# A one-token decoder block: wq in one load over all 128 partitions, and the last rows of w_down as two loads of 128 rows

## The chip, the cores and the metric

The kernel runs on one core of a Trainium2 chip. The metric is the device time of one execution in microseconds (us); shorter is better. Everything is stored in bf16; the sums are kept in fp32.

## What is computed

One token with 640 features passes through an attention block with a cache of 4096 positions and 32 heads of 128 features, and then through a gated feed-forward block with 1728 hidden features. `A_x` is x; `B_x` isn't used.

```python
q = (layernorm(x) @ wq)                       # 640 x 4096, 32 heads of 128
p = softmax(q . k_cache * 128 ** -0.5)        # 32 heads, 4096 positions
h = x + (p @ v_cache) @ wo                    # 4096 x 640
g = layernorm(h) @ w_gate                     # 640 x 1728
u = layernorm(h) @ w_up                       # 640 x 1728
out = h + (gelu(g) * u) @ w_down              # 1728 x 640
```

Nearly all of the input is read once: K and V are 33.6 MB each, wq and wo 5.2 MB each, the three matrices of the feed-forward block 2.2 MB each, 84.2 MB in all.

## The kernel before, in words

The program is written as one list of operations for each engine, with explicit dependencies (`Prog`, lines 33 to 90). `P.dma` (line 50) puts a load on the list of the engine that issues it; all but the load of x are issued by SyncE (SP), in the order in which they stand in the code. An operation that depends on another waits on a semaphore (line 84) before it is issued, and everything behind it on that engine waits too. A DMA counts as done when its semaphore has reached 16 (line 90). SP's queue thus holds the loads in a fixed order, and a load that waits for a buffer holds up all those behind it.

**Start.** SP issues wq first (lines 156 to 158), into `arena`, a buffer of 40 KB in each partition. Five successive rows of wq go to one partition, so partition p gets 40,960 contiguous bytes. The load is split in two: partitions 0 to 15 (640 KB) and partitions 16 to 127 (4480 KB). Meanwhile VectorE and GpSimd write constants, and a small layernorm of x is done (lines 212 to 231). The matrix multiply `q_proj` (lines 236 to 243) waits for the layernorm and for both loads of wq; it makes q for all heads, repeated over 32 partitions for each of four heads, and VectorE and ScalarE copy it to `qb` (lines 244 and 245).

**The stream of K and V.** The heads are taken in eight groups of four. K of a group is one load of 4096 KB over 128 partitions (32 partitions for each head, 32 KB a partition), V as well; the last V is in two halves. There are three slots of memory for these loads, and the order is K0, K1, V0, K2, V1, and so on (`order`, lines 159 to 162). `issue` (line 172) puts the next load on SP's list with a wait for the last use of its slot; the first three wait for nothing and are issued behind wq. For each quarter of a K load, VectorE multiplies K by q (line 254), TensorE folds the 128 features to 16 by adding eight slices in PSUM (line 262), VectorE sums those 16 (line 269), and ScalarE takes the exponentials (line 273). TensorE then multiplies them with V (line 291) and adds up the partial sums of the heads (line 300).

**The rest.** When the last K and V loads have been put on the list, SP issues wo in three loads into `arena` (lines 360 to 362), which is free once q is made. The matrices of the feed-forward block go into the slots of the last K and V loads (lines 363 to 378): first the last 192 rows of w_down, in two loads (128 rows into column 12 of `wd_sb`, 64 rows into partitions 0 to 63 of column 13), then w_gate, w_up in two pieces, and the first 1536 rows of w_down in three. The first of them waits for the last use of its slot (`free[1]`).

The hidden features lie in 14 columns of 128: `glu` (line 392) computes gate and up by 5 x 14 matmuls of 128 by 128 each into one column of PSUM at a time; the fourteenth column has 64 features, so its matmuls are half as wide and fill only half of the partitions. Two memsets (lines 380 and 381) put zeros in the other half, since the gelu (lines 414 to 422) works on whole columns. `down` (line 424) multiplies each column by its 128 rows of w_down, or by the 64 rows in the last column, in four quarters of 160 outputs, columns 12 and 13 first, then the others in the order in which they land. Two copies each on VectorE and ScalarE and a store end the program.

Of the kernel before, what the change touches and what calls it, by code (L numbers as in the profile page):

```python
# [92 lines left out]
def bass_sequential_preLN__gqa_block_cached__glu_gated_geglu__decode_kernel(nc, A_x, A_k_cache, A_v_cache, A_wq, A_wo, B_x, B_w_gate, B_w_up, B_w_down, out):  # L93
# [3 lines left out]
    arena = sb("arena", [128, 5 * 4096], BF16)  # L97
# [13 lines left out]
    hlnT = sb("hlnT", [128, 5], BF16)  # L111
# [12 lines left out]
    hm = sb("hm", [128, 14], BF16)  # L124
# [10 lines left out]
    ps_g, ps_u = bank[0], bank[1]  # L135
    ps_q = [bank[3], bank[7]]
    ps_a = bank[3]
    ps_d = bank[3][:, 256:416]
# [8 lines left out]
    P = Prog(nc)  # L147
    V = lambda fn, *d: P.op("vector", fn, *d)
# [4 lines left out]

    d_x = P.dma("scalar", x_row[:, :], A_x[0, :, :])
    A(lambda e: e.preload_act_table_set("natural_log_exp_and_others"))
    wq_v = A_wq[:, :].rearrange("(p c) n -> p (c n)", c=5)
    d_wq = [P.dma("sync", arena[0:16, :], wq_v[0:16, :]),
            P.dma("sync", arena[16:128, :], wq_v[16:128, :])]
    order = [("K", 0)]
    for G in range(NG - 1):  # L160
        order += [("K", G + 1), ("V", G)]
# [86 lines left out]
    folds, reds, exps, pvs, evs, hds = {}, {}, {}, {}, {}, {}  # L248
# [76 lines left out]
    def proj_part(t, lo, hi, *ws):  # L325
        def fn(e):
            for c in range(5):
                for i in range(lo, hi):
                    r = e.matmul(ps_p[:, c:c + 1], wo_sb[:, t, i, c::5], aP[:, t, i:i + 1],  # L329
                                 start=(t == 0 and c == 0 and i == 0), stop=(t == 1 and i == 15),  # L330
                                 skip_group_check=True)
            return r
        return T(fn, *ws)
# [11 lines left out]
    for G in range(NG):  # L345
# [6 lines left out]
        if G == 4:  # L352
# [14 lines left out]
    wd_sb = sl[1][:, 0:14 * D].rearrange("p (m n) -> p m n", m=14)  # L367
# [1 line left out]
    wd_v = B_w_down[0:1536, :].rearrange("(a p r) n -> p a r n", a=3, r=4)  # L369
    wd_d = wd_sb[:, 0:12, :].rearrange("p (a r) n -> p a r n", a=3)  # L370
    d_wd = [P.dma("sync", wd_sb[:, 12, :], B_w_down[1536:1664, :], free[1]),
            P.dma("sync", wd_sb[0:64, 13, :], B_w_down[1664:1728, :])]
    d_wg = P.dma("sync", wg_sb, B_w_gate[:, :].rearrange("(p c) n -> p c n", c=5), free[0])
    d_wu = [P.dma("sync", wu_sb[:, 0:3, :], wu_v[:, 0:3, :]),
            P.dma("sync", wu_sb[:, 3:5, :], wu_v[:, 3:5, :])]
# [1 line left out]
             P.dma("sync", wd_d[:, 2, 0:2, :], wd_v[:, 2, 0:2, :]),  # L377
             P.dma("sync", wd_d[:, 2, 2:4, :], wd_v[:, 2, 2:4, :])]

    V(lambda e: e.memset(ps_g[64:128, 13:14], 0.0), reds[31])  # L380
    V(lambda e: e.memset(ps_u[64:128, 13:14], 0.0), reds[31])
    proj_part(0, 0, 16, a0, d_wo["0"])
    proj_part(1, 0, 12, a1, d_wo["1a"])
    pr = proj_part(1, 12, 16, d_wo["1b"])
# [7 lines left out]
    def glu(ps, w, cs):  # L392
        def fn(e):
            for c in cs:
                for m in range(14):
                    ws = w[:, c, 512 * (m // 4) + m % 4:512 * (m // 4) + 512:4] if m < 12 else \
                        w[:, c, 128 * m:min(128 * m + 128, DF)]
                    k = 128 if m < 13 else 64
                    i = e.matmul(ps[0:k, m:m + 1], ws, hlnT[:, c:c + 1], start=(c == 0 and m == 0), stop=(c == 4),  # L399
                                 skip_group_check=True)  # L400
            return i
        return fn
    ga = T(glu(ps_g, wg_sb, range(5)), hl, d_wg)
# [20 lines left out]
    def down(ms, last):  # L424
        def fn(e):
            for m in ms:
                k = 128 if m < 13 else 64
                for q in range(4):
                    i = e.matmul(ps_d[32 * q:32 * q + 1, 0:160], hm[0:k, m:m + 1],  # L429
                                 wd_sb[0:k, m, 160 * q:160 * q + 160],  # L430
                                 start=False, stop=(last and m == ms[-1]))
            return i
        return fn
# [41 lines left out]
```

## Time and profile before

| | us |
|---|---|
| median of 3 runs | 218.11 (217.61 to 218.71) |
| the profiled execution | 218.02 |
| its span, first to last instruction | 216.2 |

The span is what the profile sees; 1.8 us of the profiled execution's time lie outside it. The views call TensorE's matmuls PE and its weight loads PEld, VectorE DVE, ScalarE ACT and GpSimd POOL; SPq is SyncE's queue of issues. L240 is line 240 of the kernel. A row of the table of stretches has the stretch in us and its length, the busy time and the instructions of each engine, and at its end the clock granted to TensorE, the busy share of the 16 DMA engines, and the GB/s that they moved. In that table a packet's bytes and time are counted in the stretch where it begins. A row of a load has its size in KB (of 1024 bytes) and the us from its issue to its landing.

### The profile page before, as it was taken

To read this page: it belongs to the slowest core of one execution; us is meant where nothing else is said; L and a number is where in the kernel's file an instruction comes from. 1 tells how busy PE (TensorE), PEld (TensorE's weight loads), DVE (VectorE), ACT (ScalarE), POOL (GpSimd) and SP (SyncE) were. 2 spreads that over 40 slices of the span, in tenths; PEclk is the share of its full clock that TensorE was granted. 3 is DMA by queue.
4 is the path that set the end of the run, shared out by engine and by line. 5 is a ranking of instruction groups with operands and counts; after the bars stand their busy time and mean duration, and the time that the engine had idled before them with its cause. 6 is when DMAs were issued, how large, how long until landed. Compare 5 with 4: busy or idle time off the path is not lost.

```text
span 216.2 us, 2508 instructions
## 1 busy us (share of the span) xinstructions
PE 121.3 (56%) x1009; PEld 58.8 (27%) x1009; DVE 100.8 (47%) x104; ACT 61.1 (28%) x273; POOL 4.1 (2%) x12
## 2 busy tenths in 40 slices
PE   1000080573965782498186728846880979566394
PEld 1000020221321240134032413312240326266382
DVE  4100001797786950875379177627923781100221
ACT  2100001056155372046205603630660156100101
POOL 7000000000000000000000000000000000000000
PEclk9999999999699998569969967995899599965555
DMA  9999899999999999999999999999999999999992
GB/s 121 227 250 242 220 436 436 424 443 406 464 396 394 449 418 452 418 436 432 430 430 430 436 415 455 414 430 430 436 430 433 415 418 433 424 405 394 406 403 76
DMA packets 4271, 84.39 MB, mean 390 GB/s; under 512 B 482, under 2 KB 676, under 8 KB 1444
## 3 DMA queue, kind: packets, MB, share of 16 engines
q1 hardware_dynamic: 4258, 84.23, 97.2%
q8 instruction: 8, 0.13, 0.3%
q14 instruction: 3, 0.02, 0.0%
q10 hardware_dynamic: 2, 0.00, 0.0%
HBM read 84.23 MB, written 0.00 MB: 390 GB/s over the span
## 4 chain that ended last, share of the span: by engine, by line
DMA 67%; DVE 14%; PE 13%; issue 3%; SPq 2%; DVEq 0%
DMA slot<-in_A_k_cache_dram 46%; DVE prod L254 12%; DMA slot<-in_A_v_cache_dram 11%; DMA slot<-in_B_w_down_dram 10%; PE bank L262 8%; PE bank L291 3%; DVE sc L269 2%; SPq L51 2%; PE bank L300 1%; PE bank L429 1%; DVEq L445 0%; DVE out_row L438 0%; PE bank L311 0%; DVE RT L310 0%
## 5 line engine op out<-in xcount | busy, mean ns | idle before, releaser
L262 PE MATMUL bank<-prod,id_b 128*128 128x512 bf16 x256 | 75.7, 456 | 53.7 <-DVE prod L254 53.7
L254 DVE TENSOR_TENSOR prod<-slot,qb 128x4096 bf16<-128x4096 bf16 x32 | 72.4, 2285 | 31.5 <-DMA slot<-in_A_k_cache_dram 31.5
L273 ACT ACTIVATE p_bd<-sc,zero_t 32x32 bf16<-32x32 f32 x128 | 46.4, 362 | 88.9 <-DVE sc L269 87.7
L262 PEld LDWEIGHTS bank<-prod,id_b 128*128 128x128 bf16 x256 | 27.0, 113 | 102.8 <-DVE prod L254 66.5
L269 DVE TENSOR_REDUCE sc<-bank 128x32 f32<-128x512 f32 x32 | 22.0, 689 | 21.6 <-PE bank L262 21.5
L273 ACT ACTIVATION_READ_ACCUMULATOR p_bd<-sc,zero_t 32x1 f32 x128 | 23.5, 184 | 0.0
L291 PE MATMUL bank<-slot,p_bd 128*16 128x512 bf16 x256 | 17.3, 380 | 0.4 <-DMA slot<-in_A_v_cache_dram 0.4
L240 PE MATMUL bank<-arena,xlnB 128*32 128x512 bf16 x40 | 4.5, 630 | 23.0 <-DMA arena<-in_A_wq_dram 23.0
L244 DVE CAST qb<-bank 128x512 bf16<-128x512 f32 x1 | 0.7, 692 | 25.9 <-PE bank L240 25.9
L291 PEld LDWEIGHTS bank<-slot,p_bd 128*16 128x16 bf16 x256 | 9.4, 89 | 4.6 <-DMA slot<-in_A_v_cache_dram 0.9
L300 PE MATMUL bank<-po_sb,hs 128*16 128x128 f32 x64 | 8.4, 274 | 1.1 <-ACT po_sb L295 1.1
L329 PE MATMUL bank<-aP,arena 128*128 128x1 bf16 x160 | 6.7, 179 | 3.9 <-DMA arena<-in_A_wo_dram 3.9
L399 PE MATMUL bank<-hlnT,slot 128*128 128x1 bf16 (+1 forms) x140 | 6.7, 176 | 3.5 <-DMA slot<-in_B_w_gate_dram 3.5
L240 PEld LDWEIGHTS bank<-arena,xlnB 128*32 128x32 bf16 x40 | 1.6, 140 | 25.0 <-issue 25.0
L245 ACT CAST qb<-bank 128x512 bf16<-128x512 f32 x1 | 0.6, 586 | 26.4 <-PE bank L240 26.4
L329 PEld LDWEIGHTS bank<-aP,arena 128*128 128x128 bf16 x160 | 6.6, 131 | 4.0 <-DMA arena<-in_A_wo_dram 2.6
L399 PEld LDWEIGHTS bank<-hlnT,slot 128*128 128x128 bf16 (+1 forms) x140 | 6.3, 118 | 4.4 <-issue 4.1
L295 ACT COPY po_sb<-bank 128x512 f32<-128x512 f32 x8 | 4.7, 585 | 7.4 <-PE bank L291 7.4
L300 PEld LDWEIGHTS bank<-po_sb,hs 128*16 128x16 f32 x64 | 5.5, 96 | 4.5 <-issue 2.1
L225 ACT ACTIVATE ln<-ln,eps_t 128x1 f32<-128x1 f32 x2 | 0.6, 294 | 17.0 <-DVE ln L223 17.0
L385 DVE TENSOR_TENSOR hT<-xx,bank 128x5 f32<-128x5 f32 x1 | 0.2, 161 | 10.2 <-PE bank L329 10.2
L315 DVE TENSOR_SCALAR aT<-bank,rz 16x128 bf16<-16x128 f32 x2 | 0.7, 340 | 5.8 <-PE bank L300 5.8
(59 smaller groups left out, 24.6 us busy)
## 6 DMA issues: line engine op xcount, KB each, us to landing
slot<-in_A_k_cache_dram SPq DMA_DIRECT2D x8, 4096.0 KB, 22.2
slot<-in_A_v_cache_dram SPq DMA_DIRECT2D x7, 4096.0 KB, 17.5
arena<-in_A_wq_dram SPq DMA_DIRECT2D x1, 4480.0 KB, 26.7
slot<-in_A_v_cache_dram SPq DMA_DIRECT2D x2, 2048.0 KB, 20.5
arena<-in_A_wo_dram SPq DMA_DIRECT2D x1, 2560.0 KB, 27.3
slot<-in_B_w_gate_dram SPq DMA_DIRECT2D x1, 2160.0 KB, 16.6
arena<-in_A_wo_dram SPq DMA_DIRECT2D x1, 1920.0 KB, 31.5
slot<-in_B_w_up_dram SPq DMA_DIRECT2D x1, 1296.0 KB, 18.4
```

The lines of the kernel that those rows point to most:

```text
L51: ev = self.op(eng, lambda e: e.dma_start(out, in_), *deps, dma=True)
L240: i = e.matmul(ps_q[hf][32 * j:32 * j + 32, :], xlnB[:, c, :], wq_j[:, c, j, 4 * hf:4 * hf + 4, :], start=(c == 0), stop=(c == 4))
L254: m = V(lambda e: e.tensor_tensor(out=prod[:, s % 4, :, :], in0=kt[:, 32 * u:32 * u + 32, :], in1=qb[:, G, :].unsqueeze(1).to_broadcast([1 ...
L262: i = e.matmul(ps_f[s % 2][:, :], id_b[:, :], prod[:, s % 4, :, 16 * b:16 * b + 16], start=(b == 0), stop=(b == 7))
L269: reds[s] = V(lambda e: e.reduce_sum(sc[:, s % 4, :], ps_f[s % 2][:, :].rearrange("p (g d) -> p g d", d=16), axis=AX.X), folds[s], exps.ge ...
L273: x = A(lambda e, j=j: e.activation(p_bd[32 * j:32 * j + 32, G % 2, 32 * (s % 4):32 * (s % 4) + 32, j], sc[32 * j:32 * j + 32, s % 4, :], ...
L291: i = e.matmul(po[a:a + 16, :], p_bd[:, G % 2, 4 * b:4 * b + 4, :].rearrange("p g j -> p (g j)"), vt[:, 4 * b:4 * b + 4, :], start=(b < 4) ...
L295: evs[G] = A(lambda e: e.copy(po_sb[:, G % 2, :], po[:, :]), pvs[G], hds.get(G - 2))
L300: i = e.matmul(ps_a[0:16, 128 * (G // 4):128 * (G // 4) + 128], hs[:, r, 12 - 4 * g:28 - 4 * g], po_sb[:, G % 2, 128 * r:128 * r + 128], s ...
L329: r = e.matmul(ps_p[:, c:c + 1], wo_sb[:, t, i, c::5], aP[:, t, i:i + 1], start=(t == 0 and c == 0 and i == 0), stop=(t == 1 and i == 15), ...
L399: i = e.matmul(ps[0:k, m:m + 1], ws, hlnT[:, c:c + 1], start=(c == 0 and m == 0), stop=(c == 4), skip_group_check=True)
L429: i = e.matmul(ps_d[32 * q:32 * q + 1, 0:160], hm[0:k, m:m + 1], wd_sb[0:k, m, 160 * q:160 * q + 160], start=False, stop=(last and m == ms ...
```

## The change

wq becomes one load over all 128 partitions. The load of the last 64 rows of w_down becomes a load of the last 128 rows (1600 to 1727), so that its first 64 rows are ones that other columns hold already and its last 64, in partitions 64 to 127, are those that are used. The fourteenth column therefore lives in partitions 64 to 127 instead of 0 to 63: the two memsets clear partitions 0 to 63, `glu` writes its narrow matmuls to partitions 64 to 127, and `down` reads `hm` and `wd_sb` there.

```diff
-    wq_v = A_wq[:, :].rearrange("(p c) n -> p (c n)", c=5)
-    d_wq = [P.dma("sync", arena[0:16, :], wq_v[0:16, :]),
-            P.dma("sync", arena[16:128, :], wq_v[16:128, :])]
+    d_wq = [P.dma("sync", arena[:, :], A_wq[:, :].rearrange("(p c) n -> p (c n)", c=5))]
...
     d_wd = [P.dma("sync", wd_sb[:, 12, :], B_w_down[1536:1664, :], free[1]),
-            P.dma("sync", wd_sb[0:64, 13, :], B_w_down[1664:1728, :])]
+            P.dma("sync", wd_sb[:, 13, :], B_w_down[1600:1728, :])]
...
-    V(lambda e: e.memset(ps_g[64:128, 13:14], 0.0), reds[31])
-    V(lambda e: e.memset(ps_u[64:128, 13:14], 0.0), reds[31])
+    V(lambda e: e.memset(ps_g[0:64, 13:14], 0.0), reds[31])
+    V(lambda e: e.memset(ps_u[0:64, 13:14], 0.0), reds[31])
...
-                    k = 128 if m < 13 else 64
-                    i = e.matmul(ps[0:k, m:m + 1], ws, hlnT[:, c:c + 1], start=(c == 0 and m == 0), stop=(c == 4),
-                                 skip_group_check=True)
+                    i = e.matmul(ps[0 if m < 13 else 64:128, m:m + 1], ws, hlnT[:, c:c + 1],
+                                 start=(c == 0 and m == 0), stop=(c == 4), skip_group_check=True)
...
-                k = 128 if m < 13 else 64
+                k = slice(0 if m < 13 else 64, 128)
                 for q in range(4):
-                    i = e.matmul(ps_d[32 * q:32 * q + 1, 0:160], hm[0:k, m:m + 1],
-                                 wd_sb[0:k, m, 160 * q:160 * q + 160],
+                    i = e.matmul(ps_d[32 * q:32 * q + 1, 0:160], hm[k, m:m + 1], wd_sb[k, m, 160 * q:160 * q + 160],
                                  start=False, stop=(last and m == ms[-1]))
```

## The prediction

> **What bounds the kernel now.** I read the profile's first parts, then the chain of waits, then tables of stretches, then the issues of the loads one by one. The busy shares alone look balanced, with no engine near full:
>
> ```profile
> span 216.2 us, 2508 instructions
> PE 121.3 (56%) x1009; PEld 58.8 (27%) x1009; DVE 100.8 (47%) x104; ACT 61.1 (28%) x273; POOL 4.1 (2%) x12
> ...
> DMA  9999899999999999999999999999999999999992
> GB/s 121 227 250 242 220 436 436 424 443 406 464 396 394 449 418 452 418 436 432 430 430 430 436 415 455 414 430 430 436 430 433 415 418 433 424 405 394 406 403 76
> ...
> DMA 67%; DVE 14%; PE 13%; issue 3%; SPq 2%; DVEq 0%
> ```
>
> The DMA row is full from the first slice to the last but one, and the chain that ends last is two thirds transfers. The GB/s row tells what the DMA row hides: in the first five slices (5.4 us each) the DMA engines are just as busy and move half as much. The table of stretches cuts this at the landings:
>
> ```profile
> 0.00:9.30 9.30, 0.96 (x7) 0.78 (x7) 2.77 (x13) 1.87 (x3) 4.11 (x12) 1.00 0.89 141
> 9.30:28.00 18.70, 0.00 (x0) 0.00 (x0) 0.00 (x0) 0.00 (x0) 0.00 (x0) 1.00 0.99 263
> 28.00:37.60 9.60, 4.46 (x40) 1.60 (x40) 0.69 (x1) 0.59 (x1) 0.00 (x0) 1.00 1.01 437
> ...
> 0.00:28.00 28.00, 0.96 (x7) 0.78 (x7) 2.77 (x13) 1.87 (x3) 4.11 (x12) 1.00 0.96 222
> 28.00:162.00 134.00, 85.68 (x506) 35.03 (x506) 81.66 (x61) 49.68 (x231) 0.00 (x0) 0.89 1.00 429
> 185.00:191.00 6.00, 2.39 (x32) 1.20 (x32) 0.58 (x4) 0.58 (x1) 0.00 (x0) 0.99 1.01 427
> 191.00:195.60 4.60, 3.36 (x80) 3.28 (x80) 0.00 (x0) 0.00 (x0) 0.00 (x0) 0.50 0.99 395
> ```
>
> The last three columns are the clock granted to TensorE, the DMA share and GB/s. The slow stretch is that of wq, and it stands on the path: the matrix multiply that makes q waits 23.0 us for it.
>
> ```profile
> arena<-in_A_wq_dram SPq DMA_DIRECT2D x1, 640.0 KB, 8.5
> arena<-in_A_wq_dram SPq DMA_DIRECT2D x1, 4480.0 KB, 26.7
> 1.24 0.40 SPq L51 DMA_DIRECT2D arena<-in_A_wq_dram  x1
> L240 PE MATMUL bank<-arena,xlnB 128*32 128x512 bf16 x40 | 4.5, 630 | 23.0 <-DMA arena<-in_A_wq_dram 23.0
> L244 DVE CAST qb<-bank 128x512 bf16<-128x512 f32 x1 | 0.7, 692 | 25.9 <-PE bank L240 25.9
> ```
>
> Issued at 1.24, the load of 112 rows lands at 27.94. From there on the stream never stops. The chain in order of time shows the first and the last link:
>
> ```profile
> 1.70 35.95 DMA slot<-in_A_k_cache_dram
> ...
> 189.26 22.68 DMA slot<-in_B_w_down_dram
> 211.94 0.04 issue
> ```
>
> K's first group lands at 37.65, 9.71 us after wq, which is what 4096 KB (4.194 MB) take at 429 GB/s, 9.8 us. The last piece of w_down lands at 211.94, and only the last few matmuls, the copies and the store follow.
>
> **Does everything behind wq move with it?** It does if the arithmetic keeps up and no queue runs dry.
>
> ```profile
> L254 DVE TENSOR_TENSOR prod<-slot,qb 128x4096 bf16<-128x4096 bf16 x32 | 72.4, 2285 | 31.5 <-DMA slot<-in_A_k_cache_dram 31.5
> L269 DVE TENSOR_REDUCE sc<-bank 128x32 f32<-128x512 f32 x32 | 22.0, 689 | 21.6 <-PE bank L262 21.5
> 37.67 2.29 DVE L254 TENSOR_TENSOR prod<-slot,qb 128x4096 bf16<-128x4096 bf16 x1 [4.40 <-DMA slot<-in_A_k_cache_dram]
> ```
>
> A group of four heads costs VectorE (72.4 + 22.0)/8 = 11.8 us and the DMA engines 2 x 9.8 = 19.6 us (K and V), and VectorE idles 31.5 us waiting for K. The product q.K of the first group also waits 4.40 us for K, not for q: q is ready 4.5 + 0.7 us after wq lands, and K 9.7 us after it. Each of these distances is counted from the landing of wq, so an earlier landing keeps them. What was done while wq was under way is short: POOL is busy for 4.11 us and VectorE for 2.77 us of the first 9.3 us, and nothing at all runs from there to 28.0. That cover is gone only if wq landed before 9.3 us, and at full rate its 5.243 MB need 12.2 us.
>
> **What the wq edit is worth.** How long one row's packet takes now: 5120 KB in 128 rows are 40,960 bytes each. Packets are counted where they begin.
>
> ```profile
> 1.00:1.70 0.70, 0.00 (x0) 0.00 (x0) 0.51 (x5) 0.35 (x1) 0.70 (x1) 1.00 0.01 2
> ...
> 1.00:2.00 1.00, 0.00 (x0) 0.00 (x0) 0.75 (x6) 0.65 (x1) 0.93 (x2) 1.00 3.65 493
> 2.00:3.00 1.00, 0.35 (x5) 0.27 (x5) 0.47 (x1) 0.63 (x1) 1.00 (x3) 1.00 1.23 164
> ```
>
> The packets that begin from 1 to 3 us carry 493 + 164 = 657 KB, the sixteen rows of the first load, and take (3.65 + 1.23) x 16 engines = 78.1 engine-us: 4.88 us a row. In the stretch 9.3 to 28.0 it is 0.99 x 16 x 18.7 = 296 engine-us for 263 x 18.7 = 4.92 MB, so 2.47 us a row if all were wq rows. At 429 GB/s a row would take 40,960 x 16 / 429 GB/s = 1.53 us. After the change no wq load of 16 or of 112 rows exists; one load of 128 rows is left, eight rows an engine. The trace has no 128-partition load of rows this long. The nearest are K and V, 4096 KB over 128 partitions or 32 KB a partition, at 429 GB/s, and the first half of wo, 20 KB a partition:
>
> ```profile
> 162.11 22.79 DMA slot<-in_A_v_cache_dram
> ...
> 163.67 0.43 SPq L51 DMA_DIRECT2D arena<-in_A_wo_dram  x1
> ...
> arena<-in_A_wo_dram SPq DMA_DIRECT2D x1, 2560.0 KB, 27.3
> ```
>
> It lands at 190.97 behind V's last piece at 184.90, so it fills the stretch from 185 to 191 us, at 427 GB/s. The length of the piece between 20 and 32 KB makes no difference there, so I take 429 for wq's 40 KB too. The lowest rate of a stretch with 128-partition loads alone, 395 (191.0 to 195.6 us), is the other bound, 13.3 us instead of 12.2.
>
> Packets begin at about 1.8 us (almost none before 1.7); that stays. Two ways to count the gain:
> - By landings. wq and K's first group are 9.437 MB, 22.0 us at 429, so K lands at 1.8 + 22.0 = 23.8 instead of 37.65: 13.8 us earlier.
> - By bytes. Up to 28.0 the engines moved 222 x 28.0 = 6.22 MB; at 429 that is done at 1.8 + 14.5 = 16.3: 11.7 us earlier.
>
> They differ because a landing waits for the last of 16 engines while the others are already at the next load. The end of the kernel is also a landing, but 170 us later, by when other delays have mixed the engines. I take the middle, 12.7, and keep both ends.
>
> The saved issue on SP (0.40 us) buys nothing: the three loads behind it wait in the rings anyway. The one load may start as much later as it is longer to issue, 0.4 us by that same row; I count it at nothing, since the K loads of 128 rows are issued at the same price:
>
> ```profile
> 49.37 0.33 SPq L51 DMA_DIRECT2D slot<-in_A_k_cache_dram  x1
> ```
>
> **What the w_down edit costs.** It reads 64 more rows, 80 KB, and moves the 64 useful rows to partitions 64 to 127.
>
> ```profile
> 186.03 0.33 SPq L51 DMA_DIRECT2D slot<-in_B_w_down_dram  x1
> ...
> 186.41 0.53 SPq L51 DMA_DIRECT2D slot<-in_B_w_down_dram  x1
> ...
> slot<-in_B_w_down_dram SPq DMA_DIRECT2D x1, 160.0 KB, 12.1
> slot<-in_B_w_down_dram SPq DMA_DIRECT2D x1, 80.0 KB, 12.2
> 164.14 0.91 SPq L51 DMA_DIRECT2D arena<-in_A_wo_dram  x2
> arena<-in_A_wo_dram SPq DMA_DIRECT2D x1, 640.0 KB, 33.1
> ```
>
> The 128-row load lands at 198.1, the 64-row load behind it at 198.6: 0.5 us for 80 KB. The 128-row load itself came some 0.4 us after the last wo piece (issued about 164.6, landed 197.7), for twice the bytes. So the new load costs between 0.1 us less than the old and, if time goes by rows, 0.5 us more; by bytes, 82 KB at 400 GB/s, 0.2 more. I take +0.2, on the path, since w_gate, w_up and the rest of w_down queue behind it. The wait for the slot is the same one, so nothing new stands on SP. The two memsets keep their shape, and the matmuls of the 14th column keep their number (10 and 4 of the 64-row form) and only change array rows or columns:
>
> ```profile
> L399 PE MATMUL bank<-hlnT,slot x140: 164/172/215, 203.7 to 210.8; 128*128 128x1 bf16 x130, 128*64 128x1 bf16 x10
> L429 PE MATMUL bank<-slot,hm x56: 287/338/342, 211.3 to 213.6; 128*1 128x160 bf16 x52, 64*1 64x160 bf16 x4
> ```
>
> They cost nothing, hidden behind the w_down landing at 211.94; were each of the fourteen 0.05 us slower without that cover, it would be 0.7 us.
>
> Sum: -12.7 + 0.2 = -12.5. The profiled execution took 218.02 us, its span 216.2 and 1.8 around it; it lies 0.1 from the median of 218.11. So 205.5 us. Its own bounds: -13.8 - 0.1 gives 204.1, and -11.7 + 0.5 + 1.1 (the 395 rate) gives 207.9.
>
> **The rivals.** First, only part comes back. Halfway, a row of the one load takes 2.0 us (328 GB/s): 16.0 us instead of 12.2, so 209.3. Further, whatever held the 112-row load at 263 GB/s (its long rows, or where wq lies in memory) holds the one load too: its 5.243 MB take 19.9 us and wq is in at 21.7. By landings K comes at 31.5 (6.1 earlier); by bytes, at 28.0 there are 5.24 + 6.3 x 0.429 = 7.95 MB moved instead of 6.22, worth 4.0. The middle is 5.1, so 213.1 us. For it: the trace has no other load from wq. Against it: the 16-row load was twice as slow from the same tensor with the same rows, so neither sets the time alone. [...]
>
> Second, no change: the 16 engines are busy at 0.96 through the first 28 us whichever load they serve, and if the start of a program is slow by time and not by load, 6.2 MB are moved by 28.0 again and only the w_down bytes change: 218.2 us. Against it: the rate rises exactly where the wq packets end. [...]
>
> Third, slower: which sixteen rows are under way together sets the time of a row (4.88 us for the first sixteen, 2.47 later), and the new sets could be of the bad kind. Eight rows at 4.88 are 39.0 us, wq lands at 40.8, K 9.8 behind it at 50.6, 13.0 later than now: 231.2 us. It turns into a loss from (27.94 - 1.8)/8 = 3.27 us a row. Against it: the long 128-partition loads in the trace run at 395 GB/s or more, and there too sixteen engines have sixteen rows under way.
>
> **How the numbers follow.** The forecast gets 0.74, the halfway case 0.09, the 263 GB/s case 0.07, no change 0.05, slower 0.05. The predicted time is that of the first, 205.5. The range takes the first from its low end (203.9, a little under 204.1 for the spread of runs) and the halfway case, up to 210.0: 0.83. Faster by more than 0.5%, about what a measurement of this kernel can tell from no change, are the first three: 0.90; within it 0.05; slower 0.05.
>
> **What would show it.** In the changed kernel's profile the first stretch should run at some 430 GB/s from 2 us on, the q matmul start near 14.5 us, its wait for wq shrink from 23.0 to about 9, K land near 24 to 25 with VectorE still waiting some 4 us for it, the later groups keep their pitch of 19.6 us, and the last w_down landing come near 199.5. The small w_down load should land 0.4 to 0.5 us after the one before it. I am wrong if wq lands after 16 us (its rate is below 370 GB/s), or if it lands early and the chain then holds a new wait, on VectorE or PE, ahead of K loads.

## The result, and the profile after

The changed kernel takes 205.74 us (median of 4 runs, 205.60 to 206.69) against 218.41 for the kernel before (4 runs beside it): a ratio of 0.943, 95% interval 0.938 to 0.948. The profiled execution took 205.85 us, its span 204.0. The forecast was 205.5 us, inside 203.9 to 210.0.

The same rows of the changed kernel's page that were read before (span, DMA share and GB/s in 40 slices, now of 5.1 us, the chain by engine):

```profile
span 204.0 us, 2507 instructions
...
DMA  7999999999999999999999999999999999999991
GB/s 249 434 442 411 411 488 430 418 411 442 430 430 424 418 427 463 424 419 418 443 450 424 421 424 438 443 430 418 424 434 450 389 440 435 413 409 425 415 393 55
...
DMA 64%; PE 14%; DVE 14%; SPq 4%; issue 3%; DVEq 0%
```

The slow start is gone: the second slice already moves 434 GB/s. The first slice holds the 1.8 us before wq's first packet. The rest looks as before, and so does the tail. The table of stretches, cut at other places (its last three columns are TensorE's clock, the DMA share and GB/s):

```profile
0.00:2.00 2.00, 0.00 (x0) 0.00 (x0) 0.97 (x7) 0.66 (x1) 1.34 (x6) 1.00 0.96 267
2.00:9.30 7.30, 0.95 (x7) 0.77 (x7) 1.80 (x7) 1.22 (x3) 2.78 (x7) 1.00 0.87 370
9.30:14.00 4.70, 0.00 (x0) 0.00 (x0) 0.00 (x0) 0.00 (x0) 0.00 (x0) 1.00 0.97 418
...
16.00:150.00 134.00, 86.52 (x506) 35.41 (x506) 81.88 (x61) 49.82 (x231) 0.00 (x0) 0.85 1.00 430
...
0.00:16.00 16.00, 0.95 (x7) 0.77 (x7) 2.77 (x13) 1.87 (x3) 4.11 (x12) 1.00 0.93 379
...
1.00:3.00 2.00, 0.35 (x5) 0.27 (x5) 1.22 (x6) 1.28 (x1) 1.93 (x4) 1.00 1.17 328
4.00:14.40 10.40, 0.60 (x2) 0.50 (x2) 1.19 (x6) 0.59 (x2) 0.78 (x2) 1.00 1.02 441
```

The same for the 112-row load of the kernel before, from the beginning of its first row to that of its last:

```profile
5.90:24.60 18.70, 0.00 (x0) 0.00 (x0) 0.44 (x1) 0.29 (x1) 0.00 (x0) 1.00 1.03 245
```

A packet is counted where it begins, so a short stretch can show more or less than was moved in it; the last two lines of the first table and the line below it hold whole rounds of packets, in each of which an engine has one row (in the changed kernel sixteen rows begin every 1.51 us, and each takes 1.51). There the time of one row of wq can be read: DMA share x 16 engines x 40.96 KB / GB/s. In the changed kernel the first sixteen rows take 655 x 1.17 / 328 = 2.34 us, the later ones 655 x 1.02 / 441 = 1.52 us. In the kernel before it was 4.88 us for the first sixteen and 655 x 1.03 / 245 = 2.75 us for the 112 behind them. The path behind it:

```profile
16.35 4.05 PE L238 MATMUL bank<-arena,xlnB 128*32 128x512 bf16 x40 [11.27 <-DMA arena<-in_A_wq_dram]
...
1.24 24.66 DMA slot<-in_A_k_cache_dram
...
25.92 2.29 DVE L252 TENSOR_TENSOR prod<-slot,qb 128x4096 bf16<-128x4096 bf16 x1 [4.78 <-DMA slot<-in_A_k_cache_dram]
...
L252 DVE TENSOR_TENSOR prod<-slot,qb 128x4096 bf16<-128x4096 bf16 x32 | 72.4, 2284 | 31.6 <-DMA slot<-in_A_k_cache_dram 31.6
...
201.34 0.10 PEld L426 LDWEIGHTS bank<-slot,hm 128*1 128x1 bf16 x8 [0.40 <-DMA slot<-in_B_w_down_dram]
```

The q matmul starts at 16.35 instead of 28.07, K lands at 25.90 instead of 37.65 (11.75 earlier), VectorE waits for K as long as before (31.6 against 31.5 us in all), and the last eight matmuls wait for the last piece of w_down until 201.34. In the kernel before they waited until 213.52, 12.2 us later:

```profile
213.52 0.10 PEld L429 LDWEIGHTS bank<-slot,hm 128*1 128x1 bf16 x8 [0.38 <-DMA slot<-in_B_w_down_dram]
```

The last piece of V lands 11.8 us earlier (173.08 against 184.90). What was gained at wq thus reaches the end of the stream unchanged, and some 0.4 us more are gained behind V, in the loads of the last weights.

### The profile page after: what moved, and what is told of

The parts are those of the page before. It is cut to its first block, busy times and chain, and to the rows that moved or that the text cites. A ratio compares the mean times of both kernels' runs of the same rounds, so it can differ in the third digit from the quotient of the medians.

```text
span 204.0 us, 2507 instructions
## 1 busy us (share of the span) xinstructions
PE 121.1 (59%) x1009; PEld 58.9 (29%) x1009; DVE 100.9 (49%) x104; ACT 61.1 (30%) x273; POOL 4.1 (2%) x12
## 4 chain that ended last, share of the span: by engine, by line
DMA 64%; PE 14%; DVE 14%; SPq 4%; issue 3%; DVEq 0%
DMA slot<-in_A_k_cache_dram 43%; DVE prod L252 12%; DMA slot<-in_A_v_cache_dram 11%; DMA slot<-in_B_w_down_dram 10%; PE bank L260 10%; SPq L51 4%; PE bank L289 3%; DVE sc L267 2%; PE bank L298 1%; PE bank L426 0%; DVEq L441 0%; DVE out_row L434 0%; PE bank L309 0%; DVE RT L308 0%
## 5 line engine op out<-in xcount | busy, mean ns | idle before, releaser
L252 DVE TENSOR_TENSOR prod<-slot,qb 128x4096 bf16<-128x4096 bf16 x32 | 72.4, 2284 | 31.6 <-DMA slot<-in_A_k_cache_dram 31.6
L242 DVE CAST qb<-bank 128x512 bf16<-128x512 f32 x1 | 0.7, 692 | 13.8 <-PE bank L238 13.8
## 6 DMA issues: line engine op xcount, KB each, us to landing
arena<-in_A_wq_dram SPq DMA_DIRECT2D x1, 5120.0 KB, 15.4
slot<-in_B_w_gate_dram SPq DMA_DIRECT2D x1, 2160.0 KB, 15.4
```

Of the source, the lines that this page charges most:

```text
L242: qa = V(lambda e: e.tensor_copy(qb[:, 0:4, :].rearrange("p g d -> p (g d)"), ps_q[0][:, :]), qd)
L252: m = V(lambda e: e.tensor_tensor(out=prod[:, s % 4, :, :], in0=kt[:, 32 * u:32 * u + 32, :], in1=qb[:, G, :].unsqueeze(1).to_broadcast([1 ...
```

## The experiments

Two questions were open: which of the two edits gives the gain, and why a load over 16 or 112 partitions is slow. The theory was that the partitions of the rows under way at the same time set the rate. The rivals were the number or size of the loads, a cold start, and the place of wq in memory. Single runs stand beside a kernel before of 218.2 to 218.4 us, whose own runs lie between 217.2 and 219.3; where a run has an interval, it is named.

**Each edit alone.** The wq edit alone is the kernel before with one load:

```diff
-    d_wq = [P.dma("sync", arena[0:16, :], wq_v[0:16, :]),
-            P.dma("sync", arena[16:128, :], wq_v[16:128, :])]
+    d_wq = [P.dma("sync", arena[:, :], A_wq[:, :].rearrange("(p c) n -> p (c n)", c=5))]
```

> The wq edit alone. Theory (the gain is wq's alone, and 64 rows more of w_down cost their bytes): wq lands near 16 us, 205.5 us, 0 to 0.4 us below the changed kernel. Rival (the w_down load over 128 partitions takes part in the gain): over 206.5 us.

Measured: 206.41 us, ratio 0.9452 (0.9432 to 0.9473): 12.0 us less than before. It lies between the theory's time and the rival's, 0.7 above the 205.74 of the changed kernel, which were taken on another occasion. The w_down edit alone is the changed kernel with the two old wq loads:

```diff
-    d_wq = [P.dma("sync", arena[:, :], A_wq[:, :].rearrange("(p c) n -> p (c n)", c=5))]
+    d_wq = [P.dma("sync", arena[0:16, :], wq_v[0:16, :]),
+            P.dma("sync", arena[16:128, :], wq_v[16:128, :])]
```

> The w_down edit alone. Theory: wq lands at 28 us as before, 218.6 us, that is 0.2 us above the kernel before (between 0.1 below and 0.5 above). Rival (it takes part in the gain): 217.5 us or less.

Measured: 217.60 us, ratio 0.9974 (0.9954 to 0.9994). By the ratio it is 0.6 us less, by the medians 0.8, and not 0.2 more; the interval ends just below 1, and the time lies a little above the rival's mark. Both results point to a small gain from w_down, so the two versions were run again side by side.

> The changed kernel again, beside the wq edit alone on the same chip. If the w_down edit costs its bytes, it is 0 to 0.4 us above the wq edit alone; if it gains as in the run with the w_down edit alone (0.6 us), 0.4 to 0.8 us below it.

> The wq edit alone again, on the same chip as the changed kernel: 205.3 to 205.7 us if the w_down edit costs its bytes, 206.2 us or more if it gains.

Measured: 205.72 us for both edits (205.49 to 206.25, 5 runs) and 206.22 for wq alone (206.03 to 206.62, 4 runs); their ratios to the kernel before are 0.9428 (0.9398 to 0.9458) and 0.9451 (0.9422 to 0.9480), which overlap. The difference of 0.5 us has the sign of the two earlier ones (0.6 and 0.7), and by the times alone it isn't shown. The profiles show a gain of some 0.3 us. Lines of the chain (V's last piece, the last eight matmuls) and of SP's issues with their us to landing, first of this last pair's run with the 64-row load, then of the one with 128 rows:

```profile
150.92 22.15 DMA slot<-in_A_v_cache_dram
...
201.60 0.46 PE bank L427 x8
...
175.40 0.58 SPq L51 DMA_DIRECT2D slot<-in_B_w_gate_dram  x1
slot<-in_B_w_gate_dram SPq DMA_DIRECT2D x1, 2160.0 KB, 16.2
```

```profile
150.82 22.15 DMA slot<-in_A_v_cache_dram
...
201.21 0.46 PE bank L426 x8
...
174.96 1.03 SPq L51 DMA_DIRECT2D slot<-in_B_w_gate_dram  x1
slot<-in_B_w_gate_dram SPq DMA_DIRECT2D x1, 2160.0 KB, 16.3
```

From V's landing (173.07, 172.97) to w_gate's (191.60, 191.26) it is 18.5 us with 64 rows and 18.3 with 128, for 80 KB more. In the kernel before it was 203.57 - 184.90 = 18.7, in the changed kernel 191.43 - 173.08 = 18.35:

```profile
186.97 1.29 SPq L51 DMA_DIRECT2D slot<-in_B_w_gate_dram  x1
slot<-in_B_w_gate_dram SPq DMA_DIRECT2D x1, 2160.0 KB, 16.6
```

```profile
149.97 23.11 DMA slot<-in_A_v_cache_dram
176.03 0.43 SPq L51 DMA_DIRECT2D slot<-in_B_w_gate_dram  x1
slot<-in_B_w_gate_dram SPq DMA_DIRECT2D x1, 2160.0 KB, 15.4
```

So 0.2 to 0.3 us are gained by the time w_gate lands, and they stay to the end. From V's landing to the last eight matmuls it is 28.6 us in the kernel before and 28.5 in both runs of the wq edit alone, 28.3 in the changed kernel and with the w_down edit alone, and 28.2 in the changed kernel run again: in all six profiles less with 128 rows. The single packets of these traces say where it lies: a row of w_gate takes 0.70 to 0.71 us on average behind the 64-row load and 0.66 behind the 128-row load, which for eight rows an engine is about 0.35 us. Why these rows are slower no run shows, and what the times differ by beyond 0.3 us isn't placed.

**Two loads, but over all partitions.** The sizes 640 and 4480 KB are kept, the cut is by columns:

```diff
+    d_wq = [P.dma("sync", arena[:, 0:2560], wq_v[:, 0:2560]),
+            P.dma("sync", arena[:, 2560:20480], wq_v[:, 2560:20480])]
```

> wq again as two loads of 640 and 4480 KB, but cut by columns: each load goes to all 128 partitions. Theory (the partitions set the rate, not the number or the size of the loads): wq lands at 16 to 16.5 us, 205.7 us. Rival (two loads in a row, or the small first one, are what is slow): wq lands after 20 us, 210 us or more.

```profile
15.80 4.46 PE L240 MATMUL bank<-arena,xlnB 128*32 128x512 bf16 x40 [10.73 <-DMA arena<-in_A_wq_dram]
```

Measured: 205.51 us, wq in at 15.8. The number and the size of the loads are not what was slow. (The time at which wq is in is here and below the start of the q matmul.)

**Half of the partitions at a time:**

```diff
+    d_wq = [P.dma("sync", arena[64 * i:64 * i + 64, :], wq_v[64 * i:64 * i + 64, :]) for i in range(2)]
```

> wq as two loads of 64 rows, partitions 0 to 63 and 64 to 127. [...] Rival (only the 16-row load was held up by its partitions, and 112 or 64 rows are as good as 128): wq lands near 16.5 us, 206 us.

```profile
4.80:25.30 20.50, 0.28 (x2) 0.18 (x1) 0.83 (x3) 0.59 (x2) 0.00 (x0) 1.00 1.08 224
...
29.19 4.17 PE L239 MATMUL bank<-arena,xlnB 128*32 128x512 bf16 x40 [24.11 <-DMA arena<-in_A_wq_dram]
```

Measured: 218.39 us, wq in at 29.2. The direction is the theory's, the size isn't: a row takes 655 x 1.08 / 224 = 3.16 us, not the 2.4 to 2.9 (211 to 215 us for the kernel) that I had worked out from half of 4.88; the half was an estimate of mine. With two equal halves the whole gain is gone.

**Sixteen rows at a time, three ways.** First into 16 partitions in a row, then into 16 partitions eight apart, then into 16 in a row but from rows eight apart in memory:

```diff
+    # 16 in a row
+    d_wq = [P.dma("sync", arena[16 * i:16 * i + 16, :], wq_v[16 * i:16 * i + 16, :]) for i in range(8)]
+    # partitions eight apart
+    d_wq = [P.dma("sync", arena[i::8, :], wq_v[16 * i:16 * i + 16, :]) for i in range(8)]
+    # rows of wq eight apart
+    d_wq = [P.dma("sync", arena[16 * i:16 * i + 16, :], wq_v[i::8, :]) for i in range(8)]
```

> wq as eight loads of 16 rows, each to 16 partitions in a row. [...] Rival (only the first load of a program is slow, since it starts cold): 1.5 us a row from the second load on, wq lands near 19 us, 209 us.

> wq as eight loads of 16 rows, each to 16 partitions that lie eight apart; the rows of a load are neighbours in memory as in the run with 16 partitions in a row. The rows of wq thus land in other partitions than the multiply by q expects: the work is the same, q is another. [...] Rival (the rows' place in memory sets it): 4.9 us a row, wq lands at 38 to 43 us, 229 to 234 us.

> wq as eight loads of 16 rows, each to 16 partitions in a row, but from rows of wq that lie eight apart in memory; rows land in other partitions than the multiply by q expects, so q is another. Theory (the partitions set the rate): 4.9 us a row, wq lands at 38 to 43 us, 229 to 234 us. Rival (the rows' place in memory sets it): 2.9 us a row or less, wq lands before 26 us, below 216 us.

One stretch and the q matmul of each, in the same order:

```profile
6.00:42.30 36.30, 0.00 (x0) 0.00 (x0) 0.44 (x1) 0.19 (x1) 0.00 (x0) 1.00 1.11 126
...
49.13 3.93 PE L239 MATMUL bank<-arena,xlnB 128*32 128x512 bf16 x40 [44.05 <-DMA arena<-in_A_wq_dram]
```

```profile
4.30:25.10 20.80, 0.60 (x2) 0.50 (x2) 0.95 (x4) 0.59 (x2) 0.48 (x2) 1.00 1.07 221
...
28.98 4.02 PE L239 MATMUL bank<-arena,xlnB 128*32 128x512 bf16 x40 [23.90 <-DMA arena<-in_A_wq_dram]
```

```profile
6.00:42.30 36.30, 0.00 (x0) 0.00 (x0) 0.44 (x1) 0.20 (x1) 0.00 (x0) 1.00 1.05 123
...
48.20 4.35 PE L239 MATMUL bank<-arena,xlnB 128*32 128x512 bf16 x40 [43.12 <-DMA arena<-in_A_wq_dram]
```

Measured: 238.26, 218.35 and 237.50 us; wq in at 49.1, 29.0 and 48.2; 5.77, 3.17 and 5.59 us a row. The order of the rows in memory changes a row's time by 3%, the partitions change it by almost half, and a cold start is ruled out, since the slow rows go on through 42 us. All three are slower than expected (229 to 234, 211 to 215 and 229 to 234 us), since a row in the long run takes more than the first sixteen rows of a program did (4.88 us).

**Another source, same partitions.** The two old loads read the K cache in place of wq:

```diff
+    wq_v = A_k_cache[0, 0:5, :, :].rearrange("h s d -> (h s d)").rearrange("(p n) -> p n", p=128)
```

> The kernel before, but the two loads to partitions 0 to 15 and 16 to 127 read the first five heads of the K cache in place of wq, 40,960 bytes a partition as before; wq is left out, so q is another. Theory (the partitions set the rate, whatever is read): the loads land at 28 us, 218.4 us. Rival (wq itself, where it lies in memory, is slow unless it is read in one load): they land before 20 us, below 211 us.

```profile
9.30:25.00 15.70, 0.00 (x0) 0.00 (x0) 0.00 (x0) 0.00 (x0) 0.00 (x0) 1.00 1.00 250
...
28.60 4.46 PE L240 MATMUL bank<-arena,xlnB 128*32 128x512 bf16 x40 [23.52 <-DMA arena<-in_A_k_cache_dram]
```

Measured: 218.75 us, in at 28.6. It isn't wq.

**Why 112 partitions are slow.** If engine by engine the 112 rows go out in blocks of seven, the rows under way at one time lie seven partitions apart; that they do is an assumption, since the traces don't show a packet's partition. Such sets of sixteen were loaded one by one:

```diff
+    d_wq = [P.dma("sync", arena[i:112:7, :], wq_v[i:112:7, :]) for i in range(7)]
+    d_wq += [P.dma("sync", arena[112:128, :], wq_v[112:128, :])]
```

> wq as seven loads of 16 rows to partitions seven apart (0, 7, ... 105, and so on, 112 partitions in all), then one of 16 rows to partitions 112 to 127; every row still lands in its own partition. [...]

```profile
4.30:9.00 4.70, 0.60 (x2) 0.50 (x2) 0.95 (x4) 0.59 (x2) 0.48 (x2) 1.00 1.19 279
9.00:12.40 3.40, 0.00 (x0) 0.00 (x0) 0.00 (x0) 0.00 (x0) 0.00 (x0) 1.00 0.70 193
12.40:14.00 1.60, 0.00 (x0) 0.00 (x0) 0.00 (x0) 0.00 (x0) 0.00 (x0) 1.00 1.18 410
14.00:19.00 5.00, 0.00 (x0) 0.00 (x0) 0.00 (x0) 0.00 (x0) 0.00 (x0) 1.00 1.10 262
19.50:21.30 1.80, 0.00 (x0) 0.00 (x0) 0.00 (x0) 0.00 (x0) 0.00 (x0) 1.00 2.69 364
...
28.16 4.46 PE L240 MATMUL bank<-arena,xlnB 128*32 128x512 bf16 x40 [23.08 <-DMA arena<-in_A_wq_dram]
```

Measured: 216.99 us, in at 28.2. If most rows took 2.3 to 3.2 us, 214 to 219 us were expected, and 206 to 211 if most took 1.5. By packets, 32 rows begin in the first line (loads 2 and 3), 16 in the second (load 4), 16 in the third (load 5), 32 in the fourth (loads 6 and 7) and 16 in the last (the neighbours). Their rows take 2.80, 2.38, 1.89, 2.75 and 4.84 us on average. Of loads 6 and 7 not a few rows are slowed but all: by the single packets of the trace the fastest of the 32 took 2.41 us and the slowest 2.91, against 1.52 with 128 partitions, and in the kernel before no row of the 112 took less than 1.94. The engines don't change to the next load at the same moment: in the kernel before the first of the 112 rows begins at 5.9 us, and the last of the sixteen rows ahead of them ends at 7.8. So rows of two loads are under way together for a part of the time, and the figure for a load is not quite that of its own sixteen partitions. Why loads 4 and 5 are faster than the others no run shows.

## Why the prediction was right, and where it wasn't

**What was slow.** Right: the chain depends on the rate of the wq load, and the partitions set that rate. The rows now stand in a series: 1.52 us with 128 partitions (from the second round on), 3.17 with 64 in a row or with 16 eight apart, 5.6 to 5.8 with 16 in a row, or in GB/s at full share 655/1.52 = 431, 655/3.17 = 207 and 655/5.7 = 115. How many partitions a load has doesn't give its rate: the load to 112 partitions ran at 245 GB/s, little above the 224 of a load to 64, and sixteen rows took 3.17 or 5.77 us each by where they went. The 112-row load goes together with the sets of sixteen seven apart, if it goes out in blocks of seven: its packets, sixteen by sixteen, take 3.41, 2.85, 2.25, 2.47, 2.63, 2.82 and 2.76 us on average, all but the first in or near the 1.89 to 2.80 of the sets. Why some sets of partitions are slower than others no run shows.

The prediction's 2.47 us a row for this load was too low: in its stretch, 9.3 to 28.0 us, the shorter rows of K begin at 25.4, and the 112 rows alone take 2.75.

**The rivals.** The halfway case did not come: a row took 1.52 us, not 2.0. Long rows alone hold nothing up, since the one load has the same rows of 40 KB. Two more are ruled out: a cold start by the eight loads of sixteen, the source by the K cache. The second, no change, did not come either, and the busy engines alone don't tell the rate: in the stretches of whole rounds behind the first sixteen rows the DMA shares were 1.02 to 1.11 for 128, 112, 64 and 16 rows alike, at 441, 245, 224 and (16 in a row) 123 to 126 GB/s. The third rival's price was real: sixteen neighbours at a time cost 20 us, where 13 had been worked out. Its case didn't occur: the one load of 128 rows ran at 1.52 us a row.

**The size of the wq term.** I took 12.7 us, between 13.8 by landings and 11.7 by bytes. Alone it measured 12.0, and K landed 11.75 earlier. The count by landings was the step that failed. It let wq and K run at 429 GB/s from 1.8 us up to K's landing, at 23.8; K landed at 25.90. And it took the lead of the fast engines over the last one for an effect of the slow load, but that lead is there after the change too. By 16.0 us the engines had begun 379 x 16.0 = 6.06 MB, 0.82 MB more than wq, when wq landed at 16.2; before it was 6.22 - 5.24 = 0.98 MB at 28.0. The first sixteen rows also took 2.34 us and not 1.53, 0.8 us that no term of the sum had. For these two reasons wq landed at 0.80 + 15.4 = 16.2 and not near 14.5, though its later rows ran at 1.52 us as forecast. The prediction had named a landing after 16 us as a sign of being wrong, since it meant a rate below 370 GB/s; the landing came later than that, though from the second sixteen rows on the rate was 441, so the mark was wrong.

```profile
0.80 0.38 SPq L51 DMA_DIRECT2D arena<-in_A_wq_dram  x1
...
arena<-in_A_wq_dram SPq DMA_DIRECT2D x1, 5120.0 KB, 15.4
```

**The rigid shift.** Right: the 31.6 us that VectorE waits for K, its 72.4 us of products and the 430 GB/s of the stream are those of before, and no new wait stands in the chain. The forecast of 199.5 for the last w_down landing took the wrong piece (211.94 is the last but one in the kernel before, since the last eight matmuls wait on to 213.52); like for like it moved by 12.2.

**The w_down term.** Wrong in sign: +0.2 was forecast, the profiles give -0.3 and the three comparisons of times -0.5 to -0.8. Its interval (-0.1 to +0.5) was built from the landing of the small load alone. That load cost no more than forecast, but the rows of w_gate behind it became faster (0.66 us against 0.70 to 0.71), for which the sum had no term. The two errors, 0.7 too much for wq and 0.5 to 1.0 too little for w_down, cancel by luck; the total is closer than its parts.

## What to carry to other kernels

Read GB/s beside the DMA share: sixteen busy engines at half the rate (a share of 1.03 at 245 GB/s, against 1.02 at 441) were here the sign that the time went by the partitions of the rows under way. Try a load over all 128 partitions, and if it has to be cut, a cut by columns before one by partitions: here the columns took 205.51 us and two halves of 64 partitions 218.39. Here even reading 64 rows of w_down twice for that cost nothing (0.3 us less by the profiles). And in a kernel that streams from beginning to end, count a gain in bytes moved and not in landings: here wq's landing waited for the slowest engine in either version, and by then the engines had begun 0.98 MB of what follows in the kernel before and 0.82 MB in the changed one; the bytes gave 11.7 us, the landings 13.8, and 12.0 came.

## What the runs showed that was not expected

A load over 112 of 128 partitions is hardly better than one over 64 (2.75 against 3.2 us a row). The loads of sixteen seven apart differ among themselves: two take a quarter to over a half longer a row on average than 128 partitions do (1.89 and 2.38 us against 1.52), four some 80% longer (2.75 to 2.80). Sixteen neighbours are faster as the first rows of a program than later (4.88 us in the kernel before, 5.77 in the long run); with 128 partitions it is the other way round (2.34 and 1.52). And two halves of 64 partitions (218.39 us) cost as much as the split into 16 and 112 (218.3).
